# Turning attention probabilities in two row tiles of 64 queries, with ScalarE's copies moved ahead of the exponentials

## The chip, the cores and the metric

The kernel runs on one core of a Trainium2 chip. TensorE (PE in the profile) multiplies matrices and can write only to the accumulator memory (PSUM, eight banks per partition); VectorE (DVE) and ScalarE (ACT) do the element work and copy results out of PSUM; GpSimd (POOL) and SyncE (SP) mostly issue transfers. The metric is the device time of one execution in microseconds, the median of several runs. Less is better.

## The reference, cut to what matters

Attention over 4 batches and 8 heads (576 positions, head size 64, a bias computed from relative position), then a two-layer network with a smooth gate on the 2304 resulting rows of 512 numbers.

```python
scores = scale * np.matmul(q, k.transpose(0, 1, 3, 2)) + bias.transpose(2, 0, 1)[None, :, :, :]
scores = scores - np.max(scores, axis=-1, keepdims=True)
attn = np.exp(scores)
attn = attn / (np.sum(attn, axis=-1, keepdims=True) + 1e-09)
out = np.matmul(attn, v)
...
h = x @ w_in
sp = np.where(h > 20.0, h, np.log1p(np.exp(np.minimum(h, 20.0))))
g = h * np.tanh(sp)
return g @ w_out
```

The product `attn @ v` sums over the keys, so TensorE needs the probabilities with keys on the partitions, while the scores come out with queries on the partitions. Each block of probabilities is therefore transposed on TensorE. All of that is float32.

## The kernel before, in words

The kernel has three stages: a bias stage (up to about 64 us), the attention stage (about 64 to 320 us) and the network stage (to the end). The change is in the attention stage.

Attention works on 16 pairs of heads (4 pairs of heads times 4 batches). A pair takes five steps, one for each chunk of queries, in the order `ORDER = [0, 1, 4, 2, 3]`: four chunks `c < 4` of 128 queries, and chunk 4, which holds the last 64 queries of both heads in one tile. That makes 80 steps. Instructions are issued in the order in which the code is written, one queue per engine; engines wait for each other only through tiles and their buffers.

Step n issues, in this order:

- `scores(n)` (line 224): twelve TensorE matmuls for a chunk below 4. The two heads lie on partitions 0 to 63 and 64 to 127, so the matmuls of the two heads use two row tiles of 64 rows ("64*128" in the profile) and start side by side. Chunk 4 takes six matmuls over all 128 rows ("128*128").
- `add_bias(n)` (line 238): VectorE adds the bias and finds the row maximum, once per head, from PSUM tile `s` into `pt`. Tile `s` has two buffers, and a chunk below 4 uses both.
- `exps(n, 0)` and `exps(n, 1)` (line 253): ScalarE takes the exponentials in place in `pt`, with the row sums.
- `transposes(n - 2)` (lines 299 to 318): TensorE turns the probabilities of two steps earlier into PSUM tiles `tp` (three buffers of one bank each), and ScalarE copies them into `main` and `tail`. A chunk below 4 has eight main blocks of 128 queries by 128 keys (line 299) and one tail block (line 302); chunk 4 has four main blocks (line 311) and two small tails (lines 315 and 316). In every fifth step the reciprocals of the sums are turned as well (line 305).
- `pv_duo` (lines 331 and 335): TensorE multiplies `main` and `tail` with the values. The two heads use two column tiles of 64 columns ("128*64"). VectorE then copies the result `x` out (line 338).
- the work of later steps: loads, the split of q and k (line 191), and pieces of the conversion of network weights (lines 112 to 151).

In a transpose the block of probabilities is the stationary operand, which TensorE loads first (LDWEIGHTS, engine PEld in the profile), and the identity matrix `ident` is the moving operand. The rows of the block are the rows of the array that it occupies, and the number of moving columns equals the number of queries in the block.

Of the kernel before, what the change touches and what calls it, by code (L numbers as in the profile page):

```python
# [7 lines left out]
F32 = mybir.dt.float32  # L8
# [11 lines left out]
P = 128  # L20
# [24 lines left out]
def kernel(ctx: ExitStack, tc, qk, v, wb, w2, w_in, w_out, psia, psi4, rinv, eye, out):  # L45
    nc = tc.nc
    pe, dve, act, pool, sp = nc.tensor, nc.vector, nc.scalar, nc.gpsimd, nc.sync
# [23 lines left out]
    ident = const.tile([P, P], F32, name="ident")  # L71
# [143 lines left out]
    def scores(n):  # L215
        i, c = steps[n]
        hi, lo = qk_hi[i], qk_lo[i]
        live[n] = [s_ps.tile([P, 2, 512], F32, name="s") for _ in range(2 if c < 4 else 1)]
        for k, (stat, mov) in enumerate(((hi, hi), (hi, lo), (lo, hi))):
            for j in range(2):  # L220
                for h in range(2 if c < 4 else 1):
                    rows = slice(h * 64, h * 64 + 64) if c < 4 else slice(0, P)
                    k0 = KO + (0 if h else 64) + j * SH
                    pe.matmul(live[n][h][:, j, :SH], stat[rows, c * P:(c + 1) * P], mov[rows, k0:k0 + SH],  # L224
                              start=(k == 0), stop=(k == 2))

    def add_bias(n):

        i, c = steps[n]
        bt = bias_t[i // B, c]  # L230
        m = st.tile([P, 2], F32, name="m")
        if c < 4:
            pt = pp.tile([P, 2 * S], F32, name="pt")
        else:
            pt = p4p.tile([P, 640], F32, name="pt4")[:, :S]
        for u, s in enumerate(live[n]):
            sl = slice(u * S, (u + 1) * S)
            dve.tensor_tensor_reduce(  # L238
                out=halves(pt[:, sl]), in0=s[:, :, :SH], in1=halves(bt[:, sl]),
                scale=-0.125, scalar=BIG, op0=ALU.add, op1=ALU.min, accum_out=m[:, u:u + 1])  # L240
        live[n] = (pt, m)

    def exps(n, u):

        i, c = steps[n]
        if u == 1 and c == 4:
            return
        if i not in sums:
            sums[i] = st.tile([P, 9], F32, name="sums", bufs=3)
        pt, m = live[n]  # L250
        ps = pt[:, u * S:(u + 1) * S]
        k = 4 * u + c if c < 4 else 8
        act.activation(ps, ps, AF.Exp, bias=m[:, u:u + 1], scale=-1.0, accum_out=sums[i][:, k:k + 1])  # L253

    def reciprocals(i):

        r = sums.pop(i)
        dve.tensor_scalar(r, r, 1e-9, None, op0=ALU.add)
        dve.reciprocal(r, r)
        return r  # L260
# [3 lines left out]
    def store_reciprocals():  # L264
        i, tp = turned.pop()
        hp, b = divmod(i, B)
        rt = rt_first.pop() if rt_first else rt_tile()
        dve.tensor_copy(rt, tp[0:9, P:2 * P])
        sp.dma_start(out=r_d[b][hp], in_=rt)

    def pt_tiles(grp):
        w = 256 if grp == 0 else 320
        main = ptp.tile([P, 2, 4, w], F32, name=f"main{grp}")
        tail = tails[grp].pop() if tails.get(grp) else tail_tile(grp)
        return main, tail[:, :w]
# [7 lines left out]
    def x_tile():  # L283
        return xs.tile([P, 320], F32, name="x", bufs=2)

    def transposes(n):
        i, c = steps[n]
        pt, m = live.pop(n)
        grp = 0 if c < 2 else 1
        if (i, grp) not in pt_t:  # L290
            pt_t[i, grp] = pt_tiles(grp)
        main, tail = pt_t[i, grp]
        if c < 4:
            off = c * P if grp == 0 else 64 + (c - 2) * P
            for h in range(2):
                tp = t_ps.tile([P, 512], F32, name="tp")
                for k in range(4):
                    c0 = h * 640 + k * P
                    pe.transpose(tp[:, k * P:(k + 1) * P], pt[:, c0:c0 + P], ident)  # L299
                (dve.tensor_copy if n < 2 and h else act.copy)(main[:, h, :, off:off + P], tp.rearrange("p (k q) -> p k q", k=4))  # L300
            tp = t_ps.tile([P, 512], F32, name="tp")
            pe.transpose(tp[:, :P], pt[:, 512:640], ident)  # L302
            r = rc.pop(n, None)
            if r is not None:
                pe.transpose(tp[0:9, P:2 * P], r, ident)
                turned.append((i, tp))
            act.copy(tail[:, off:off + P], tp[:, :P])
        else:
            tp = t_ps.tile([P, 512], F32, name="tp")
            for k in range(4):  # L310
                pe.transpose(tp[:, k * P:(k + 1) * P], pt[:, k * P:(k + 1) * P], ident)  # L311
            act.copy(main[:, :, :, 0:64].rearrange("p h k q -> p k h q"),
                     tp.rearrange("p (k h q) -> p k h q", k=4, h=2))
            tp = t_ps.tile([P, 512], F32, name="tp")
            pe.transpose(tp[0:64, P:2 * P], pt[:, 512:S], ident)
            pe.transpose(tp[:, :P], pt[:, S - P:S], ident)
            act.copy(tail[0:64, 0:64], tp[0:64, P:P + 64])
            act.copy(tail[64:128, 0:64], tp[64:128, 64:128])
# [30 lines left out]
    blocks = [(0, 512), (512, 512), (1024, 256), (1280, 512), (1792, 512)]  # L349
# [25 lines left out]
    def ahead(n):  # L375

        i, x = divmod(n, 5)
        if x == (1 if i else 4) and i + 2 < NPAIR:
            load_hi(i + 2)
            load_raw(i + 2)  # L380
        if x == 4 and i + 2 < NPAIR:
            load_v(i + 2)
        if i % B == B - 1 and i // B + 1 < HP:
            load_bias(i // B + 1, ORDER[x])
        if n == NS - 11:
            load_x(0, x0)
        if n in (NS - 10, NS - 6):
            x_r[0] = x0.tile([P, 2, TB], F32, name="xr", bufs=1)
            h0 = 0 if n == NS - 10 else 2
            load_r(0, x_r[0], h0, h0 + 2)  # L390
        if n in (NS - 7, NS - 3):
            h0 = 0 if n == NS - 7 else 2
            for d in range(2):
                pool.tensor_tensor(x_raw[0][:, h0 + d], x_raw[0][:, h0 + d], x_r[0][:, d], op=ALU.mult)

    def split(n):

        i, x = divmod(n, 5)
        if (x == 2 or n == 3) and i + 1 < NPAIR:
            split_qk(i + 1)  # L400
        if w32:
            lower_weights(dve)
        if half:
            parts.pop(0)()
        elif n > 5 and w64[0][0] in order[:HALF]:
            scale_high(act if x == 2 else dve)
            parts.extend((shift_low, merge, lambda: (sign(), cast_weights())))

    def step(n):
        i, x = divmod(n, 5)  # L410
        late = n == 4

        def begin():
            if n < NS:
                scores(n)
                add_bias(n)
                exps(n, 0)

        def end():
            if n < NS:  # L420
                exps(n, 1)
                ahead(n)
            if 0 <= n - 1 < NS and (n - 1) % 5 == 4:
                rc[n - 1] = reciprocals((n - 1) // 5)
            if n < NS:
                split(n)
            if turned:
                store_reciprocals()


        if not late:
            begin()
        for k in {3: (0, 1)}.get(n, (n - LAG,)):
            if 0 <= k < NS:
                transposes(k)
        if not late:
            end()

        if late:
            for k in range(5):  # L440
                pv_duo(0, 0, k)
        for j, grp, ks in {4: ((i, 0, (0, 1)),), 0: ((i - 1, 0, (2, 3)),), 1: ((i - 1, 0, (4,)),),
                           2: ((i - 1, 1, (0, 1, 2)),), 3: ((i - 1, 1, (3, 4)),)}[x]:
            if 0 <= j < NPAIR and (j, grp) != (0, 0):
                for k in ks:
                    pv_duo(j, grp, k)
        if late:
            begin()
            end()
# [26 lines left out]
    def reach(t):  # L476

        left, right = 16 * t + 15, S - 16 * t
        n = max(left + 1, right)
        return left, right, n + n % 2  # L480
# [12 lines left out]
    for idx in range(NB + 2):  # L493
# [4 lines left out]
        if idx + 2 < NB:  # L498
            n = reach(ts[idx + 2])[2]
# [82 lines left out]
    t_ps = lpsum("t_ps", 3)  # L582
# [248 lines left out]
```

## Time and profile before

| what | value |
|---|---|
| median of 3 runs | 720.19 us (719.24 to 720.92) |
| the profiled execution | 721.65 us, span 719.7 us |
| TensorE busy | 697.3 us, 97% of the span |
| VectorE busy | 515.3 us, 72% |
| ScalarE busy | 467.2 us, 65% |
| granted TensorE clock, mean | 0.995 of full speed |

The span runs from the first to the last instruction. The time of the execution has about 2 us more around it. The profiled execution is 1.46 us above the median of the runs, so a sum made against the profile has to be carried over to the median.

### The profile page before, as it was taken

What the parts mean: (1) busy time and instruction counts of PE and PEld (TensorE: products, weight loads), DVE (VectorE), ACT (ScalarE), POOL (GpSimd) and SP (SyncE); (2) the same over time, 40 slices, a digit from 0 to 9 for tenths busy, and PEclk for the clock granted to TensorE, in tenths of its full rate; (3) what the DMA queues carried; (4) which work ended last, traced back from release to release, by engine and by line L of the source; (5) the groups of instructions that cost most, each with busy time, mean ns of one, the idle gap of its engine ahead of it and who ended that gap; (6) DMA issues with size and microseconds to landing.
All of it is one profiled execution on the core that took longest, in us unless ns stands there. A gap on an engine that the chain in (4) does not pass through costs nothing.

```text
span 719.7 us, 12986 instructions
## 1 busy us (share of the span) xinstructions
PE 697.3 (97%) x4880; PEld 532.4 (74%) x4880; DVE 515.3 (72%) x1051; ACT 467.2 (65%) x964; POOL 16.5 (2%) x26
## 2 busy tenths in 40 slices
PE   6988999999999999988999999999999999999997
PEld 3546776677677676656878888889988888888886
DVE  7894777777777876547888888775675567565564
ACT  6985888888888888845565565654554554454443
POOL 1000000000000001100000000000100000000000
PEclk9999999999999999999999999999999999999999
DMA  8989568548655844251113321214131000010001
GB/s 258 287 270 308 207 189 272 164 152 266 233 185 171 289 148 143 57 156 38 58 60 118 93 83 58 71 48 118 59 98 49 1 0 1 0 59 1 0 1 59
DMA packets 46430, 86.85 MB, mean 121 GB/s; under 512 B 13200, under 2 KB 22048, under 8 KB 46368
## 3 DMA queue, kind: packets, MB, share of 16 engines
q1 hardware_dynamic: 43488, 75.32, 32.5%
q0 software_dynamic: 2304, 10.49, 4.7%
q8 instruction: 38, 0.62, 0.4%
q10 hardware_dynamic: 576, 0.22, 0.1%
q14 instruction: 24, 0.20, 0.1%
HBM read 64.56 MB, written 21.45 MB: 120 GB/s over the span
## 4 chain that ended last, share of the span: by engine, by line
PE 86%; DVE 7%; ACT 4%; issue 1%; DMA 1%; DVEq 0%; ACTq 0%; SPq 0%
PE y L675 24%; PE h L630 24%; PE s L224 11%; PE o L331 9%; PE tp L299 8%; PE bps L528 5%; PE o L335 2%; PE tp L311 1%; PE tp L302 1%; DVE e L653 1%; DMA rawqk<-in_qk_dram 1%; DVE e L637 1%; DVE e L652 1%; ACT bt L534 1%; DVE w L127 1%
## 5 line engine op out<-in xcount | busy, mean ns | idle before, releaser
L253 ACT ACTIVATE pt<-pt,m 128x576 f32<-128x576 f32 x144 | 112.7, 782 | 40.8 <-DVE m L238 39.6
L238 DVE CUSTOM_DVE_ANT_0 pt<-s,bias 128x576 f32<-128x576 f32 x144 | 103.7, 753 | 47.4 <-PE s L224 47.4
L675 PE MATMUL y<-who,ghi 128*128 128x512 f32 x288 | 112.5, 391 | 2.2 <-ACT ghi L654 1.4
L675 PE MATMUL y<-who,glo 128*128 128x512 f32 x288 | 112.4, 390 | 1.0 <-DVE glo L657 1.0
L654 ACT CAST ghi<-e 128x512 fp32r<-128x512 f32 x72 | 44.7, 621 | 105.1 <-DVE e L653 101.9
L675 PE MATMUL y<-wlo,ghi 128*128 128x512 f32 x288 | 112.2, 390 | 0.0
L630 PE MATMUL h<-xhi,whi 128*128 128x512 f32 (+1 forms) x320 | 79.7, 369 | 1.3 <-ACT xhi L605 1.2
L657 DVE TENSOR_TENSOR glo<-e,ghi 128x512 fp32r<-128x512 f32 x72 | 49.7, 690 | 42.0 <-ACT ghi L654 42.0
L630 PE MATMUL h<-xlo,whi 128*128 128x512 f32 (+1 forms) x320 | 79.5, 371 | 0.0
L630 PE MATMUL h<-xhi,wli 128*128 128x512 f32 (+1 forms) x320 | 79.4, 370 | 0.0
L331 PE MATMUL o<-main,vt 128*64 128x320 f32 (+1 forms) x512 | 75.8, 418 | 0.8 <-DVE x L338 0.8
L635 ACT ACTIVATE e<-h 128x512 f32<-128x512 f32 x72 | 42.7, 592 | 46.2 <-PE h L630 46.2
L299 PE MATMUL tp<-ident,pt 128*128 128x128 f32 x512 | 70.0, 280 | 1.2 <-ACT main L300 1.2
L636 DVE TENSOR_SCALAR e<-e 128x512 f32<-128x512 f32 x72 | 30.6, 425 | 56.1 <-ACT e L635 56.1
L300 ACT COPY main<-tp 128x512 f32<-128x512 f32 x126 | 66.9, 581 | 1.0 <-PE tp L299 0.6
L630 PEld LDWEIGHTS h<-xhi,whi 128*128 128x128 f32 x320 | 57.3, 188 | 13.6 <-ACT xhi L605 2.7
L630 PEld LDWEIGHTS h<-xlo,whi 128*128 128x128 f32 x320 | 57.5, 190 | 10.2
L675 PEld LDWEIGHTS y<-who,ghi 128*128 128x128 f32 x288 | 54.1, 188 | 14.3 <-ACT ghi L654 2.2
L630 PEld LDWEIGHTS h<-xhi,wli 128*128 128x128 f32 x320 | 57.2, 190 | 10.1
L299 PEld LDWEIGHTS tp<-ident,pt 128*128 128x128 f32 x512 | 56.5, 142 | 10.3 <-issue 3.1
L675 PEld LDWEIGHTS y<-who,glo 128*128 128x128 f32 x288 | 54.1, 188 | 13.5 <-DVE glo L657 2.3
L675 PEld LDWEIGHTS y<-wlo,ghi 128*128 128x128 f32 x288 | 54.1, 188 | 10.9
(73 smaller groups left out, 1017.7 us busy)
## 6 DMA issues: line engine op xcount, KB each, us to landing
bias_d<-bt SPq DMA_DIRECT2D x36, 295.5 KB
qkhi<-in_qk_dram POOLq DMA_DIRECT2D x16, 640.0 KB, 6.2
rawqk<-in_qk_dram SPq DMA_DIRECT2D x16, 640.0 KB
w<-in_w_in_dram SPq DMA_DIRECT2D x16, 512.0 KB
w<-in_w_out_dram SPq DMA_DIRECT2D x16, 512.0 KB
vt<-in_v_dram SPq DMA_DIRECT2D x16, 320.0 KB
bias<-bias_d SPq DMA_DIRECT2D x16, 288.0 KB
out_dram<-w SPq DMA_DIRECT2D x17, 256.0 KB
```

The lines of the kernel that those rows point to most:

```text
L224: pe.matmul(live[n][h][:, j, :SH], stat[rows, c * P:(c + 1) * P], mov[rows, k0:k0 + SH], start=(k == 0), stop=(k == 2))
L238: dve.tensor_tensor_reduce(out=halves(pt[:, sl]), in0=s[:, :, :SH], in1=halves(bt[:, sl]), scale=-0.125, scalar=BIG, op0=ALU.add, op1=ALU. ...
L253: act.activation(ps, ps, AF.Exp, bias=m[:, u:u + 1], scale=-1.0, accum_out=sums[i][:, k:k + 1])
L299: pe.transpose(tp[:, k * P:(k + 1) * P], pt[:, c0:c0 + P], ident)
L300: (dve.tensor_copy if n < 2 and h else act.copy)(main[:, h, :, off:off + P], tp.rearrange("p (k q) -> p k q", k=4))
L331: pe.matmul(o[h * 64:h * 64 + 64, :w], vt[:, h, k, :], main[:, h, k, :], start=(k == 0), stop=False, **kw)
L528: pe.matmul(ps[cg * 32:cg * 32 + 32, a:b], w2t, src, start=True, stop=True)
L630: pe.matmul(h[:, u * n:(u + 1) * n], w["i", g4, d][:, r * P:(r + 1) * P], x[:, d, :n], start=(k == 0), stop=(k == 11))
L635: act.activation(e, h, AF.Exp)
L654: act.copy(ghi, e)
L657: dve.tensor_tensor(glo, e, ghi.bitcast(F32), op=ALU.subtract)
L675: pe.matmul(ys[blk][t], g[:, c0:c0 + P], w, start=((blk, f) in first and k == 0), stop=((blk, f) in last and k == 2))
```

## The change

Three things change. First, the main blocks are no longer turned 128 queries at a time: `turn_blocks` cuts each block into its upper 64 and its lower 64 queries, turns each half with a 64 by 64 piece of the identity, and puts the upper halves of all blocks into one `tp` tile and the lower halves into another. The halves alternate. Second, the copies out of the two `tp` tiles are now split by half instead of by head (for chunk 4, by head instead of all at once). Third, `exps(n, 0)` moves from the beginning of a step to its end, so ScalarE makes the copies of step n - 2 first and then both exponentials of step n.

```diff
+    ROWS = (slice(0, 64), slice(64, P))
+
+    def turn_blocks(pt, cols):
+
+        ab = [t_ps.tile([P, 512], F32, name="tp") for _ in ROWS]
+        for k, c0 in enumerate(cols):
+            for rows, tp in zip(ROWS, ab):
+                pe.transpose(tp[:, k * 64:(k + 1) * 64], pt[rows, c0:c0 + P], ident[rows, rows])
+        return [tp[:, :len(cols) * 64].rearrange("p (k q) -> p k q", q=64) for tp in ab]
+
     def transposes(n):
...
-            for h in range(2):
-                tp = t_ps.tile([P, 512], F32, name="tp")
-                for k in range(4):
-                    c0 = h * 640 + k * P
-                    pe.transpose(tp[:, k * P:(k + 1) * P], pt[:, c0:c0 + P], ident)
-                (dve.tensor_copy if n < 2 and h else act.copy)(main[:, h, :, off:off + P], tp.rearrange("p (k q) -> p k q", k=4))
+            blocks = main.rearrange("p h k q -> p (h k) q")
+            for u, tp in enumerate(turn_blocks(pt, [h * 640 + k * P for h in range(2) for k in range(4)])):
+                (dve.tensor_copy if n < 2 and u else act.copy)(blocks[:, :, off + 64 * u:off + 64 * u + 64], tp)
...
         else:
-            tp = t_ps.tile([P, 512], F32, name="tp")
-            for k in range(4):
-                pe.transpose(tp[:, k * P:(k + 1) * P], pt[:, k * P:(k + 1) * P], ident)
-            act.copy(main[:, :, :, 0:64].rearrange("p h k q -> p k h q"),
-                     tp.rearrange("p (k h q) -> p k h q", k=4, h=2))
+            for h, tp in enumerate(turn_blocks(pt, range(0, 512, P))):
+                act.copy(main[:, h, :, 0:64], tp)
...
                 scores(n)
                 add_bias(n)
-                exps(n, 0)
...
             if n < NS:
+                exps(n, 0)
                 exps(n, 1)
```

On TensorE, two neighbouring steps in the middle of the attention stage (a chunk below 4 being turned, then chunk 4) stand like this before. `s` are scores, `tp` turned blocks, `o` the product with the values; the shape is that of the output, and a product `o` counts once here although the profile shows two instructions for it.

```order
L224 MATMUL s<-qkhi,qklo 128x288 x4
L299 MATMUL tp<-ident,pt 128x128 x8
L302 MATMUL tp<-ident,pt 128x128
L331 MATMUL o<-main_3721,vt 64x320 x2
L335 MATMUL o<-tail_3722,vt 64x320 x2
...
L224 MATMUL s<-qkhi,qklo 128x288 x4
L311 MATMUL tp<-ident,pt_3854 128x128 x4
L315 MATMUL tp<-ident,pt_3854 64x128
L316 MATMUL tp<-ident,pt_3854 128x128
```

With the change the same place reads as follows.

```order
L224 MATMUL s<-qkhi,qklo 128x288 x4
L293 MATMUL tp<-ident,pt 128x64 x16
L309 MATMUL tp<-ident,pt 128x128
L335 MATMUL o<-main_4154,vt 64x320 x2
L339 MATMUL o<-tail_4155,vt 64x320 x2
...
L224 MATMUL s<-qkhi,qklo 128x288 x4
L293 MATMUL tp<-ident,pt_4310 128x64 x8
L319 MATMUL tp<-ident,pt_4310 64x128
L320 MATMUL tp<-ident,pt_4310 128x128
```

Eight transposes over 128 rows became sixteen over 64 rows with half as many moving columns (and four became eight); their place between the scores and the tail is the same.

On ScalarE, two steps in the same part of the program stand like this before (`pt` lines are exponentials, `main` and `tail` lines copies).

```order
L253 ACTIVATE pt,sums<-pt,m 128x576
L300 COPY main_4177<-tp 128x4x128 x2
L307 COPY tail_4178<-tp 128x128
L253 ACTIVATE pt,sums<-pt,m 128x576 x2
L300 COPY main_4177<-tp 128x4x128 x2
L307 COPY tail_4178<-tp 128x128
L253 ACTIVATE pt,sums<-pt,m 128x576
```

With the change, the corresponding steps of a neighbouring pair read as follows.

```order
L307 COPY main_4686<-tp 128x8x64 x2
L314 COPY tail_4687<-tp 128x128
L253 ACTIVATE pt,sums<-pt,m 128x576 x2
L307 COPY main_4686<-tp 128x8x64 x2
L314 COPY tail_4687<-tp 128x128
L253 ACTIVATE pt,sums<-pt,m 128x576 x2
```

The first exponential of a step moved behind the step's three copies. Each copy of `main` still moves 512 elements per partition, now as eight runs of 64 instead of four of 128.

## Rows read from the trace of the kernel before

**Rows 1.** The page: TensorE's busy time, share of span, instructions.

```profile
PE 697.3 (97%) x4880; PEld 532.4 (74%) x4880; DVE 515.3 (72%) x1051; ACT 467.2 (65%) x964; POOL 16.5 (2%) x26
```

**Rows 2.** Busy time by stretch: length, engines, granted clock, DMA share, GB/s.

```profile
68.00:306.00 238.00, 237.79 (x2041) 167.15 (x2038) 175.10 (x435) 202.25 (x514) 11.39 (x16) 0.99 0.59 193
326.00:719.00 393.00, 386.27 (x1786) 321.43 (x1784) 278.68 (x460) 203.62 (x341) 2.60 (x2) 1.00 0.15 49
```

**Rows 3.** Timeline of TensorE, two steps: start us, us, instruction, count.

```profile
200.96 0.43 PE L224 MATMUL s<-qkhi,qklo 128*128 128x288 f32 x2
201.22 1.03 PE L299 MATMUL tp<-ident,pt 128*128 128x128 f32 x8
202.09 0.27 PE L302 MATMUL tp<-ident,pt 128*128 128x128 f32 x1
...
204.09 0.53 PE L224 MATMUL s<-qkhi 64*128 64x288 f32 x4
204.47 0.42 PE L224 MATMUL s<-qklo,qkhi 64*128 64x288 f32 x4
204.73 0.42 PE L224 MATMUL s<-qkhi,qklo 64*128 64x288 f32 x4
205.08 1.09 PE L299 MATMUL tp<-ident,pt 128*128 128x128 f32 x8
206.01 0.27 PE L302 MATMUL tp<-ident,pt 128*128 128x128 f32 x1
206.22 0.76 PE L331 MATMUL o<-main,vt 128*64 128x320 f32 x4
206.81 0.71 PE L335 MATMUL o<-tail,vt 128*64 128x320 f32 x4
207.44 0.53 PE L224 MATMUL s<-qkhi 64*128 64x288 f32 x4
```

**Rows 4.** The same timeline, a product of 256 moving columns.

```profile
209.25 1.08 PE L331 MATMUL o<-main,vt 128*64 128x256 f32 x8
210.26 0.53 PE L224 MATMUL s<-qkhi 64*128 64x288 f32 x4
```

**Rows 5.** The same timeline, tail block and then nine columns of reciprocals.

```profile
215.33 0.27 PE L302 MATMUL tp<-ident,pt 128*128 128x128 f32 x1
215.44 0.27 PE L305 MATMUL tp<-ident,sums 128*9 128x128 f32 x1
```

**Rows 6.** Timeline of weight loads: first and second of two kinds of scores, second transpose.

```profile
200.32 0.30 PEld L224 LDWEIGHTS s<-qkhi 128*128 128x128 f32 x2 [0.38 <-DVE m L238]
200.43 0.19 PEld L224 LDWEIGHTS s<-qkhi 128*128 128x128 f32 x1
...
204.20 0.19 PEld L224 LDWEIGHTS s<-qkhi 64*128 64x128 f32 x2
...
205.14 0.14 PEld L299 LDWEIGHTS tp<-ident,pt 128*128 128x128 f32 x1
```

**Rows 7.** Groups of instructions: the main transposes; count, busy us, mean ns, idle.

```profile
L299 PE MATMUL tp<-ident,pt 128*128 128x128 f32 x512 | 70.0, 280 | 1.2 <-ACT main L300 1.2
```

**Rows 8.** Timeline of ScalarE in one step without waiting.

```profile
186.95 0.78 ACT L253 ACTIVATE pt<-pt,m 128x576 f32<-128x576 f32 x1
...
187.72 1.05 ACT L300 COPY main<-tp 128x512 f32<-128x512 f32 x2
188.67 0.28 ACT L307 COPY tail<-tp 128x128 f32<-128x128 f32 x1
```

**Rows 9.** Timeline of VectorE: both heads' bias in one step.

```profile
205.19 0.76 DVE L238 CUSTOM_DVE_ANT_0 pt<-s,bias 128x576 f32<-128x576 f32 x1 [0.50 <-PE s L224]
...
206.55 0.08 DVE L238 DVE_READ_ACCUMULATOR2_ANT m<- 128x1 f32 x1
```

**Rows 10.** Waits from 75 to 325 us: who for whom, us, times, longest.

```profile
ACT pt L253 <- DVE m L238: 32.3, 56, 1.3
```

**Rows 11.** Timeline of TensorE at the end of the attention stage.

```profile
308.93 2.06 PE L630 MATMUL h<-xhi,whi 128*128 128x512 f32 x4 [1.22 <-ACT xhi L605]
```

## The prediction

> **What bounds the kernel now.** First the page: TensorE is busy for 97% of the span [rows 1]. Then the busy times by stretch, since an average hides stages. From 68 to 306 us, where the change lies, TensorE is busy for 237.79 of 238.00 us, ScalarE for 202.25 and VectorE for 175.10, at a granted clock of 0.99 [rows 2]; from 326 us on nothing changes. These 238 us are 15 pairs of heads, 15.87 us each. A busy TensorE may still be a waiting one, because the time of a matmul is longer than its place in the array. So the third view is TensorE's timeline: one must look at when the next instruction starts, not at how long one takes. There the step's instructions follow each other without a wait for another engine [rows 3]. What TensorE's queue loses or gains in this stage is therefore the first estimate of the result, until ScalarE or VectorE cannot follow.
>
> **What a main transpose costs today.** Eight start at 201.22 and the tail at 202.09: 0.109 us each [rows 3]. The price goes by the moving columns. The tail, with the same 128 moving columns, also holds the array for 0.11 us although the load behind it has only nine columns [rows 5], so the weight loads are hidden. A product over two column tiles says the same: 320 moving columns take 1.22 us for four pairs (206.22 to 207.44), 256 take 1.01 us (209.25 to 210.26) [rows 3, 4], so 64 float32 columns cost 0.053 us per pair, and two tiles pay it together.
>
> **What a pair of halves will cost.** No row shows a float32 transpose in row tiles, so both its parts are bounded. Do two row tiles run side by side? The scores do: four over 64 rows take 0.26 us (204.47 to 204.73), as do two over 128 rows (200.96 to 201.22) [rows 3]. So a pair of halves has 64 moving columns to pay once, 0.053 to 0.055 us. The loads: the second transpose's load starts 0.06 us after the first (205.08, 205.14) [rows 3, 6], which is what one full load of float32 takes when nothing hides it. Do two half-height loads take as long as one full one? For scores they do: the second full load starts 0.11 us after the first (200.32, 200.43), and with two row tiles the second pair starts 0.11 us after the first pair (204.09, 204.20) [rows 3, 6]. I take a price p of 0.058 us per pair, between the columns (0.055) and the load (0.060). The lower end is 0.053; the upper end, with loads or matmuls strictly one after another, 0.11 to 0.12.
>
> **Where the switch of tile shape goes.** Transposes over 128 rows start 0.09 us late behind scores over 64 rows (205.08 instead of 204.73 + 0.26), and their first load adds 0.06 us (0.93 us for eight, 206.01 - 205.08, against 0.87); behind scores over 128 rows neither appears [rows 3]. I price a switch at 0.15 us. The Trainium skill, page "TensorEngine Tiling (Array Packing)", section Key Properties, says that changing the tiling mode drains TensorE; by that rule too, the 128-row tail behind the 64-row halves pays for a switch. The trace agrees, with the 0.09 us; were the tail's switch free, the sum below would be 80 x 0.15 = 12 us larger. So:
> - Blocks of chunks 0 (at their own place, below), 1, 2 and 3: for the three that follow 64-row scores, the switch moves from ahead of the main blocks to behind them. Gain 0.87 - 8p, 48 times.
> - Chunk 0 is turned behind the 128-row scores of chunk 4, where there is no switch now and will be two. Gain 0.87 - 8p - 0.30, 16 times.
> - Chunk 4, four blocks: 0.436 - 4p, 16 times.
>
> Together the 80 steps give 57.9 - 576p us: **24.5 us at p = 0.058**, 27.4 at 0.053, nothing at 0.10, and 5.5 to 11 us lost at 0.11 to 0.12. The 512 records of line 299 [rows 7] are the 64 eights in it.
>
> **ScalarE.** Its copies of 512 elements keep their price (1.05 us for two, 0.28 for the tail [rows 8]), in runs of 64 instead of 128. For chunk 4 one copy becomes two of 256 elements, each between 0.28 and 0.53 us; at 0.36 each that is 0.2 us more per pair of heads, 3 us in all on ScalarE. The moved exponential costs nothing by itself. Today ScalarE waits 32.3 us for VectorE's maximum, 56 times [rows 10], with the copies queued behind that wait; now the copies fill that time. The exponentials finish later in their step, but are read two steps later. A step's work is two exponentials of 0.78 us at most and copies of 1.33 us at most, 2.9 us with all overlaps counted twice; the mean over the stretch has to do: 202.25 + 3 us of work in 238 - 24.5 = 213.5 us, 96%. Part of the 202 us is the start-up of instructions after the 56 waits, which goes with them. It fits, but barely, and it is the cover under which the gain stands: without it a lag of ScalarE reaches TensorE through the `tp` buffers. Both halves now need two free banks before the first pair, where the second bank was needed four blocks later.
>
> **VectorE.** The scores of the next step need both buffers of `s`. A step's scores start at 204.09, VectorE starts at 205.19 and is done with both heads at 206.63 [rows 3, 9]: a loop of 2.54 us. The step from 207.44 to 210.26 [rows 3, 4], which turns chunk 4, shrinks from 2.82 to 2.62 us, still above the loop; the shortest step is followed by chunk 4's scores, which need one buffer alone. No loss here, but no more than 0.1 us of room either.
>
> **Ends of the stage.** The last steps are held by ScalarE (the network's first matmul waits 1.22 us for it [rows 11]), not by transposes; I take off 1 us, and 1.5 us for steps in which ScalarE is late. Gain 22 us.
>
> **The rivals.**
> - *ScalarE sets the pace.* If half of its 32.3 us of waits stays, now as waits for `tp`, its 205 us grow to 221, and only 17 of the 238 us go; less the ends, the median would be about 706. For it speaks the 96%; against it, that the copies no longer stand behind the maximum. It decides from about 0.1 us of waiting per step on.
> - *Loads are not hidden behind matmuls of the same rows.* Then today's 0.109 is a load of 0.055 and a matmul of 0.054, and a pair becomes 0.055 + 0.027 = 0.082: a gain of 10.7 us, less 1.5, about 711. The nine-column load [rows 5] speaks against it, since the block ahead of it should then have been followed after 0.06 us. The rule is that of the Trainium skill, page "TensorE: Matmul & The Clock Gate", section The mechanism: a weight load overlaps running matmuls only where the row group differs. The trace does not agree, with the 0.11 us of those rows.
> - *The halves do not overlap (the other side).* If float32 loads of two row tiles go one after the other, p is 0.11 to 0.12, sixteen loads bound the group, and the two switches at chunk 4's scores come on top: 5.5 to 11 us slower, 726 to 731. It decides from p = 0.10 on. For it speaks that no row has such float32 transposes; against it the scores, whose loads and matmuls overlap in both tiles.
>
> **How the numbers follow.** The span of 719.7 us becomes 697.7, the profiled execution's 721.65 becomes 699.65; the median of the runs lay 1.46 us below that execution, so I say 698.2 us. For this case alone, p from 0.053 to 0.065 gives 695 to 702. Chances: the forecast 0.70, ScalarE's pace 0.13, unhidden loads 0.06, no overlap 0.11. The range from 693.5 to 711 holds the first, nearly all of the second and half of the third, a little over 8 in 10. A measurement of this kernel tells about 0.2% (1.4 us) from no change: faster 0.87, same 0.03 (from the edges of the last two cases), slower 0.10.
>
> **What would show it.** In the profile after: eight pairs of halves in 0.44 to 0.52 us from the first to the switch; no gap between 64-row scores and the first half, and 0.15 us ahead of the tail; a pair of heads in about 14.3 us; ScalarE's waits for VectorE's maximum mostly gone and its busy share near 95%. A pair of halves at 0.11 us, TensorE waiting for `tp` copies in most steps, or scores waiting for VectorE's maximum would make it wrong.

## The result and the profile after

The changed kernel takes **699.89 us** (698.39 to 701.45), the kernel before 720.56 us (719.24 to 721.03) in the same comparison: a ratio of 0.9716, 95% interval 0.9691 to 0.9742, 20.7 us faster. The profiled execution took 701.45 us, with a span of 699.5 us against 719.7.

The page of the changed kernel, as in [rows 1], with its groups of ScalarE's exponentials and main copies (count, busy us, mean ns, idle time ahead and what ended most of it):

```profile
PE 675.6 (97%) x5456; PEld 515.5 (74%) x5456; DVE 514.3 (74%) x1051; ACT 463.9 (66%) x980; POOL 16.5 (2%) x26
...
L253 ACT ACTIVATE pt<-pt,m 128x576 f32<-128x576 f32 x144 | 112.5, 792 | 6.5 <-DVE m L238 6.2
...
L307 ACT COPY main<-tp 128x512 f32<-128x512 f32 x126 | 68.1, 597 | 18.4 <-PE tp L293 18.0
```

TensorE has 576 instructions more and 21.7 us less busy time. ScalarE's 32.3 us of waits for VectorE's maximum [rows 10] are down to 6.2 us; it now waits for the halves instead (18.0 us), as an engine with work to spare does.

Busy time by stretch, as in [rows 2]: the attention stage from 68 us, now to 284 us; the rest of the kernel; and the start of the stage:

```profile
68.00:284.00 216.00, 215.74 (x2572) 150.91 (x2572) 172.68 (x434) 198.47 (x525) 11.41 (x16) 0.98 0.65 212
304.00:699.00 395.00, 388.05 (x1794) 322.92 (x1793) 279.58 (x462) 204.68 (x343) 2.60 (x2) 1.00 0.15 49
54.00:75.00 21.00, 16.04 (x176) 12.72 (x169) 10.39 (x26) 10.89 (x29) 0.53 (x1) 0.84 0.97 324
```

TensorE is still busy in all of the stage, and behind the stage nothing changed. In this execution the start of the stage lost something; it is read further down.

TensorE's timeline in two steps of the changed kernel, the same places of the loop as in [rows 3]:

```profile
190.45 0.43 PE L224 MATMUL s<-qkhi,qklo 128*128 128x288 f32 x2
190.81 0.71 PE L293 MATMUL tp<-ident,pt 64*128 64x64 f32 x16
191.45 0.33 PE L309 MATMUL tp<-ident,pt 128*128 128x128 f32 x1
191.71 1.83 PE L335 MATMUL o<-main,vt 128*64 128x320 f32 x12
193.47 0.53 PE L224 MATMUL s<-qkhi 64*128 64x288 f32 x4
193.84 0.42 PE L224 MATMUL s<-qklo,qkhi 64*128 64x288 f32 x4
194.11 0.43 PE L224 MATMUL s<-qkhi,qklo 64*128 64x288 f32 x4
194.37 0.66 PE L293 MATMUL tp<-ident,pt 64*128 64x64 f32 x16
194.96 0.33 PE L309 MATMUL tp<-ident,pt 128*128 128x128 f32 x1
195.21 0.76 PE L335 MATMUL o<-main,vt 128*64 128x320 f32 x4
195.80 0.71 PE L339 MATMUL o<-tail,vt 128*64 128x320 f32 x4
196.44 0.53 PE L224 MATMUL s<-qkhi 64*128 64x288 f32 x4
```

Read the starts. A half is one transpose of 64 queries, and a pair is one half in each row tile. Behind 64-row scores the halves follow without a gap (194.11 + 0.26 = 194.37). The sixteen starts lie within 0.435 us, seven intervals of 0.062 us, and the tail starts 0.154 us after the last pair, one interval and 0.09 us of switch: 0.59 us in all. Behind 128-row scores (190.45) there is the switch too: 0.36 us to the halves instead of 0.26, and 0.64 us from the first half to the tail, 0.05 of it the first load. The step from 193.47 to 196.44 takes 2.97 us, where it took 3.35 (204.09 to 207.44 in [rows 3]).

Why 0.062 us: the last pair of the group at 190.81, its loads and its matmuls, changed kernel:

```profile
191.24 0.14 PEld L293 LDWEIGHTS tp<-ident,pt 64*128 64x128 f32 x2
191.29 0.23 PE L293 MATMUL tp<-ident,pt 64*128 64x64 f32 x2
```

A half's load starts some 0.005 us after the matmul ahead of it (191.23, one interval before 191.29), and its own matmul follows about 0.055 us later. So I read that loads, not columns, set the pace; no run changes one without the other. The first two pairs of loads of that group start 0.056 us apart with nothing to hide them, where two full loads start 0.06 us apart (205.08 and 205.14 in [rows 3, 6]): loads of both tiles together take what one full load takes.

ScalarE's timeline in the same step of the changed kernel:

```profile
193.11 0.84 ACT L253 ACTIVATE pt<-pt,m 128x576 f32<-128x576 f32 x1
...
195.06 1.07 ACT L307 COPY main<-tp 128x512 f32<-128x512 f32 x2 [1.01 <-PE tp L293]
196.01 0.28 ACT L314 COPY tail<-tp 128x128 f32<-128x128 f32 x1
196.17 0.80 ACT L253 ACTIVATE pt<-pt,m 128x576 f32<-128x576 f32 x1
```

The copies come first and wait 1.01 us for the halves, and the exponential follows the tail's copy at once: the maximum has long been there.

### The profile page after: what moved, and what is told of

It is laid out like the page before. It is cut to its first block, busy times and chain, and to the rows that moved or that the text cites. A ratio compares the mean times of both kernels' runs of the same rounds, so it can differ in the third digit from the quotient of the medians.

```text
span 699.5 us, 14139 instructions
## 1 busy us (share of the span) xinstructions
PE 675.6 (97%) x5456; PEld 515.5 (74%) x5456; DVE 514.3 (74%) x1051; ACT 463.9 (66%) x980; POOL 16.5 (2%) x26
## 4 chain that ended last, share of the span: by engine, by line
PE 85%; DVE 7%; ACT 3%; DMA 3%; issue 1%; SPq 0%; DVEq 0%; ACTq 0%
PE y L679 25%; PE h L634 24%; PE s L224 11%; PE o L335 10%; PE tp L293 5%; PE bps L532 5%; PE o L339 2%; PE tp L309 2%; DMA rawqk<-in_qk_dram 1%; DMA xlo<-r_d 1%; DVE e L657 1%; DVE e L641 1%; DVE e L656 1%; ACT bt L538 1%; DVE w L127 1%
## 5 line engine op out<-in xcount | busy, mean ns | idle before, releaser
L657 DVE TENSOR_TENSOR e<-e,r 128x512 f32<-128x512 f32 x72 | 49.9, 693 | 7.5
L224 PEld LDWEIGHTS s<-qkhi 64*128 64x128 f32 (+1 forms) x288 | 25.0, 189 | 36.9 <-DVE m L238 16.2
```

What stands on the lines that cost most here:

```text
L657: dve.tensor_tensor(e, e, r, op=ALU.mult)
```

## The experiments

Each ratio is to the kernel before, timed on the same chip; the runs are spread over several chips, so ratios are compared and not only times. The theory: two row tiles turn a pair of blocks in about the time of one load, and ScalarE's new order is what lets it follow. The rivals differ by run.

**1. The tiles without the new order.** In the changed kernel:

```diff
                 add_bias(n)
+                exps(n, 0)
 ...
-                exps(n, 0)
                 exps(n, 1)
```

> The row tiles as in the change, but the first exponential of a step stands ahead of the copies again, as before the change. Theory (TensorE's queue sets the pace, and the moved exponential is the cover under which ScalarE can follow): ScalarE waits for VectorE's maximum ahead of the copies again, 32 us of waits beside some 200 us of work do not fit into the 216 us that TensorE now leaves, so TensorE waits for copies and part of the gain is lost: 704 to 716 us. Rival (the order costs nothing, only the tiles count): 699 to 701 us.

Measured 711.57 us (709.26 to 712.63), 0.9883 [0.9852, 0.9914], in the theory's range. The new order is worth 12 of the 20.7 us; a pair of heads takes 15.11 us here and 14.40 in the changed kernel. The waits of this kernel from 75 to 292 us (who for whom, us, times, longest):

```profile
ACT pt L253 <- DVE m L238: 23.3, 37, 1.5
...
PEld tp L293 <- ACT main L307: 7.9, 26, 0.4
```

and TensorE's timeline in one of its steps:

```profile
208.30 0.27 PE L293 MATMUL tp<-ident,pt 64*128 64x64 f32 x1
208.79 0.71 PE L293 MATMUL tp<-ident,pt 64*128 64x64 f32 x15 [0.21 <-ACT main L307]
```

ScalarE waits for the maximum again, its copies behind that wait are late, and the lateness comes out at the halves: the first has its bank, its partner in the other tile waits for the second bank, and fourteen wait behind it. That both banks are wanted before the first pair is the new sensitive point.

**2. The new order without the tiles.** The same line moved the other way, in the kernel before.

> The transposes as before the change, only the first exponential moved behind the copies. Theory (TensorE's queue is full without it, so ScalarE's order has nothing to give): 719 to 722 us, with ScalarE's waits for VectorE's maximum mostly gone all the same. Rival (the order carries a good part of the gain): 705 to 716 us.

Measured 720.18 us (717.31 to 721.73), 0.9995 [0.9976, 1.0015]: nothing, as the theory says. A pair of heads takes 15.85 us as before. The waits of this kernel from 75 to 295 us:

```profile
ACT main L300 <- PE tp L299: 23.8, 31, 1.9
...
ACT main L312 <- PE tp L311: 7.2, 11, 0.7
```

ScalarE's wait of 32.3 us for the maximum [rows 10] has become 31.0 us for the transposes. This wait belongs to an engine that does not set the pace, and moving it cost and gave nothing. With the tiles it counts, because ScalarE then has 22 us less for the same work.

**3. The same halves, all of one tile first.** In `turn_blocks` of the changed kernel:

```diff
-        for k, c0 in enumerate(cols):
-            for rows, tp in zip(ROWS, ab):
+        for rows, tp in zip(ROWS, ab):
+            for k, c0 in enumerate(cols):
```

> The change, but all upper halves are turned first and all lower halves after them, instead of alternating: the same instructions in another order. Theory (the gain is that loads and matmuls of two row tiles run side by side): neighbours now share a row tile, sixteen loads follow each other at about 0.06 us, a group takes 0.99 us instead of 0.49, and 64 x 0.5 + 16 x 0.25 = 36 us come on top: 726 to 738 us. Rival (half the moving columns give half the price whatever the order, or TensorE overlaps them by looking ahead in its queue): 699 to 702 us.

Measured 718.4 us (715.27 to 719.84), 0.997 [0.9949, 0.9991]: between the ranges of the two. TensorE's timeline of one group of this kernel:

```profile
156.89 0.42 PE L224 MATMUL s<-qkhi,qklo 64*128 64x288 f32 x4
157.15 0.96 PE L293 MATMUL tp<-ident,pt 64*128 64x64 f32 x16
158.04 0.33 PE L309 MATMUL tp<-ident,pt 128*128 128x128 f32 x1
```

From the first half to the tail 0.89 us instead of 0.59: strictly one after another it would be 16 x 0.062 + 0.09 = 1.08 us. So three pairs still ran together (starts in the order of the program would allow one, the last of the upper tile with the first of the lower). The single starts of this group, in us after the first:

```
0 .055 .118 .181 .242 .248* .304 .361 .365 .423 .428 .486 .550 .612 .674 .739
```

The starts come in twos in the middle only. The one with the star takes 273 ns, where others take some 220, and lies 0.25 us after the first in the groups behind 64-row scores (0.30 where the first load is exposed). I read it as the first half of the lower tile, ninth in the program, because a tile's first half is the one that must wait for its bank: in 59 of the 64 groups of sixteen, this sixth start and the first one are the only ones that carry such a wait. So it starts with the fifth of the upper tile, ahead of the sixth to the eighth.

**4. Four of one tile, then four of the other.** In the changed kernel's `turn_blocks`:

```diff
-        for k, c0 in enumerate(cols):
+        for k4 in range(0, len(cols), 4):
             for rows, tp in zip(ROWS, ab):
+                for k, c0 in list(enumerate(cols))[k4:k4 + 4]:
```

> The change, with the halves issued four upper, four lower, four upper, four lower, instead of alternating. All eight upper ones first had cost 0.74 us for a group instead of 0.43, with the first lower half starting beside the fifth upper one. Theory (TensorE starts a matmul of the other row tile ahead of its turn when it stands up to four matmuls behind): the four lower ones start at once beside the upper ones, and the time is that of the change, 699 to 702 us. Rival (neighbours in the queue must alternate, and the overlap seen in the sequence of eight came from the end of the first tile's work): every four run alone, a group takes about 0.9 us, 722 to 732 us.

Measured 701.87 us (700.82 to 703.33), 0.9755 [0.9727, 0.9782], at the upper edge of the theory's range. TensorE's timeline of one group of this kernel:

```profile
184.38 0.72 PE L294 MATMUL tp<-ident,pt 64*128 64x64 f32 x16
185.02 0.33 PE L310 MATMUL tp<-ident,pt 128*128 128x128 f32 x1
```

0.64 us to the tail, one interval more than alternating. A pair of heads takes 14.69 us instead of 14.40, so the time is not quite that of the change: 4.8 us for sixteen pairs by the steps, 2.8 us by the ratios. Here the first half of the lower tile, fifth in the program, starts with the first of the upper (0.007 us later). Both runs fit a TensorE that starts the first matmul of the other row tile together with the one four places ahead of it in the program, while the three between them still wait. The Trainium skill, page "TensorE: Matmul & The Clock Gate", section The mechanism, has matmuls start and end strictly in the order of the program; for starts in different row tiles these two traces do not agree, by the 0.739 and 0.494 us within which the sixteen starts lie.

**5. Chunk 0's tail turned first**, behind the 128-row scores of chunk 4, which spares one of the two switches there. In `transposes` of the changed kernel:

```diff
+            if c:
+                turn_main()
             tp = t_ps.tile([P, 512], F32, name="tp")
             pe.transpose(tp[:, :P], pt[:, 512:640], ident)
 ...
             act.copy(tail[:, off:off + P], tp[:, :P])
+            if not c:
+                turn_main()
```

> The change, but where the main blocks follow chunk 4's scores over 128 rows (chunk 0's blocks, once per pair of heads), the tail block over 128 rows is turned first and the halves after it. Theory (each change of tile shape costs TensorE about 0.15 us): one switch less per pair of heads, 16 x 0.15 = 2.4 us less, 697 to 698.5 us. Rivals: the switch is free, then 699 to 701 us; or the last of the three banks, which now takes a half, comes free too late, then 700 to 703 us.

Measured 698.57 us (695.82 to 699.36), 0.9702 [0.9674, 0.973], between the ranges of the theory and of a free switch. The same kernel again, beside the changed kernel on one chip:

> The tail first behind chunk 4's scores, once more. Theory (one switch of tile shape less in each of 16 pairs of heads; the steps in the trace were shorter by 0.15 us): 2.4 us below the change on the same chip, 696 to 699.5 us. Rival (what the steps gain is lost at the ends of the stage): within 1 us of the change.

> The changed kernel once more, as it is, to stand on the same chip beside the version with the tail first. Theory: 698 to 702 us.

Measured 697.56 us (696.29 to 698.95), 0.9691 [0.9666, 0.9716], against 698.86 us (697.23 to 701.23), 0.9713 [0.9688, 0.9737] for the change. TensorE's timeline of two such steps, in the first of these runs:

```profile
131.67 0.27 PE L314 MATMUL tp<-ident,pt 128*128 128x128 f32 x1
131.87 0.90 PE L293 MATMUL tp<-ident,pt 64*128 64x64 f32 x16
132.71 1.84 PE L342 MATMUL o<-main,vt 128*64 128x320 f32 x12
...
203.03 0.43 PE L224 MATMUL s<-qkhi,qklo 128*128 128x288 f32 x2
203.29 0.27 PE L314 MATMUL tp<-ident,pt 128*128 128x128 f32 x1
203.49 0.71 PE L293 MATMUL tp<-ident,pt 64*128 64x64 f32 x16
204.13 1.84 PE L342 MATMUL o<-main,vt 128*64 128x320 f32 x12
205.90 0.53 PE L224 MATMUL s<-qkhi 64*128 64x288 f32 x4
```

The tail follows the 128-row scores without a gap (203.03 + 0.26). From these scores to the next step it takes 2.87 us, where the change takes 3.02 (190.45 to 193.47): one switch of 0.15 us less, as priced. Of the fourteen pairs of heads from the third on, eleven have it, and their step goes from 3.66 to 3.51 us. In the other three, as at 131.87, the halves take 0.84 us to the product instead of 0.64, and the step takes 3.70 us. VectorE's copies of the reciprocals in these two steps, same run, say why:

```profile
131.74 0.27 DVE L268 COPY rt<-tp 9x128 f32<-9x128 f32 x1
...
203.07 0.28 DVE L268 COPY rt<-tp 9x128 f32<-9x128 f32 x1 [0.24 <-ACT tail L319]
```

The reciprocals stand in the third `tp` bank of the step before, which with the tail first goes to the lower halves. At 203 the copy ends at 203.35, before the halves begin (203.49). At 131 it ends at 132.01: the first upper half has started at 131.87, and its partner starts at 132.06. All three late steps show this, in run 7 and in the second comparison too, so the rival of the bank that comes free too late holds in three pairs of fourteen. The mean gain is then 0.10 us per pair, 1.7 us for sixteen and not 2.4. The times show 1.3 in both comparisons, whose intervals overlap with the change's: the saving is seen in the steps, not settled in the time. This version has the lowest median of all that ran.

**6. The raw load of the second pair of heads asked for earlier.** At the start of the stage VectorE waits for a transfer. In the changed kernel:

```diff
+        if idx == 33:
+            load_raw(1)
         if idx == NB:
-            load_raw(1)
             load_v(1)
```

> The change, with one transfer moved: the q and k of the second pair of heads (rawqk) are requested three rounds earlier in the bias stage. Theory (the first microseconds that the tiles save are lost again because VectorE waits 5.04 us for that transfer at the start of the attention stage, and TensorE 3.44 us for VectorE): 696 to 699 us. Rival (the transfer engines are full at that time, so that an earlier request only pushes others back): 699 to 702 us.

Measured 702.53 us (699.88 to 706.41), 0.9768 [0.9738, 0.9799]: no gain, half a microsecond above the rival's range, and the theory of a request that comes too late has fallen. This kernel's window at the start of the stage:

```profile
54.00:75.00 21.00, 17.27 (x161) 12.69 (x154) 9.19 (x22) 9.67 (x25) 0.53 (x1) 0.70 0.86 285
```

The request went out at 54.19 instead of 57.26 us and VectorE's wait for it is down to 1.4 us, but other transfers are now late (a copy of ScalarE waits 2.3 us for a store of the bias stage, VectorE 1.2 us for the bias), and the clock granted in these 21 us is 0.70 instead of 0.84. The DMA engines of the changed kernel were 0.97 busy there, so I read that what is asked for sooner takes its turn from something else.

With the fifth edit as well:

> Both together: the tail first behind chunk 4's scores, and the transfer requested earlier. Theory (the two are independent, 2.4 us of switches and 1 to 4 us of start): 694 to 697.5 us. Rival (neither start nor switch adds to the other, or the transfer gives nothing): 698 to 701 us.

Measured 700.08 us (697.75 to 703.16), 0.973 [0.9701, 0.9758], in the rival's range. Its waits from 53 to 75 us have the bias too:

```profile
DVE pt L238 <- DMA bias<-bias_d: 2.5, 2, 1.4
```

**7. More work for ScalarE.** How near is it to setting the pace? The copy of the lower half made twice, in the changed kernel:

```diff
                 (dve.tensor_copy if n < 2 and u else act.copy)(blocks[...], tp)
+                if n >= 2 and u:
+                    act.copy(blocks[...], tp)
```

> The change, with the copy of the lower halves of every chunk below 4 (from the third step on) made twice by ScalarE, with the same result: some 62 x 0.48 = 30 us more work on ScalarE and nothing else. Theory (ScalarE is the next bound, with 198.5 us of work in the 216 us of the stage): 17.5 us of it are free, the rest lands on the time, 710 to 718 us. Rival (ScalarE still has room or the waits move elsewhere): 699 to 703 us.

Measured 722.31 us (719.04 to 724.88), 1.0035 [1.0016, 1.0055]: the mechanism of the theory, but above its range. This kernel's busy times from 75 to 290 us, and two of its waits from 75 to 295 us:

```profile
75.00:290.00 215.00, 204.67 (x2357) 138.69 (x2357) 162.84 (x400) 210.91 (x536) 9.76 (x14) 1.00 0.60 198
```

```profile
PEld tp L293 <- ACT main L309: 15.3, 29, 1.0
PE tp L293 <- ACT main L309: 9.8, 23, 0.8
```

ScalarE is busy for 98% and TensorE waits for its copies: the two rows, of loads and of matmuls, show the same waits and are not to be added. The 62 added copies made ScalarE's busy time in the stage 33.9 us longer (249.5 against 215.6 us) and the kernel 22.4 us, so some 11 us were free, not the 17.5 us (216.0 - 198.5) that the windows seem to offer. A share of 92% is a mean over five kinds of step, and ScalarE's room is not spread evenly: the step that turns chunk 0 went from 3.66 to 4.34 us (4.86 in every fourth pair of heads) and the one that turns chunk 3 from 2.43 to 3.00, while the other three grew by less than 0.1.

## Why the prediction was right

**The place and the mechanism held.** What TensorE's queue loses is the result, within 3 us: its steps lose 23.4 us (below), the time 20.7. The two rivals on the tiles are excluded by the spacing of the pairs: 0.062 us, neither 0.082 (loads unhidden) nor 0.11 to 0.12 (no overlap). ScalarE's pace is excluded as a bound of the change: in the steady steps TensorE hardly waits for a copy, and a pair of heads takes 14.40 us where 14.3 was forecast. But run 1 shows that this rival is near: without the new order the time is 711.57 us.

**The price of a switch held.** 0.15 us was read from a switch that the change moves (0.09 and a first load of 0.06); after it is 0.09 ahead of the tail, with a first load of 0.05 to 0.06, and run 5 takes one away and sees 0.15 go.

**The price of a pair, 0.058 us, was too low: 0.062.** The load at 0.060 was the nearer bound, and I put the value between the load and the columns. The sum 57.9 - 576p becomes 22.2 us, 2.3 less. The steps themselves gave a little more than that: by their place in a pair of heads, starting with chunk 4's scores, they went from 3.75 to 3.66, 3.35 to 2.97, 2.81 to 2.58, 3.14 to 2.76 and 2.81 to 2.43 us, together 1.46 per pair, or 0.29 per step and 23.4 us for 80, where the formula with 0.062 gives 22.2. Of these 1.2 us, 0.5 stand in the step that turns chunk 4 (2.81 to 2.58): the block behind its halves has 64 stationary columns instead of 128, and its first load delays it by 0.03 us (the next matmul starts 0.135 us after it, less 0.109) where the price of a switch has 0.06, sixteen times. The rest is open.

**The 1.5 us for steps in which ScalarE is late were not lost there, and the ends of the stage kept back more than 1 us.** The scores of step 79 start at 282.81 instead of 302.58 us; chunk 4's scores in the second pair of heads (step 7) start at 74.30 instead of 72.97. So the 72 steps between saved 21.1 us (0.29 each). Ahead of them five steps' blocks are turned, and 1.3 us were lost where 1.5 should have been saved, 2.8 us short. Behind them three are turned, and 0.4 us came back instead of 0.9: 24.5 - 2.3 + 1.2 - 2.8 - 0.4 = 20.2 us of span. The timeline of VectorE and TensorE at the start of the stage, changed kernel:

```profile
65.03 1.49 DVE L191 TENSOR_TENSOR qklo<-rawqk,qkhi 128x1280 fp32r<-128x1280 f32 x1 [5.04 <-DMA rawqk<-in_qk_dram]
...
67.59 0.40 PE L224 MATMUL s<-qkhi 64*128 64x288 f32 x1 [3.44 <-DVE m L238]
```

and the same instruction of VectorE in the kernel before, with its window from 54 to 75 us:

```profile
64.03 1.49 DVE L191 TENSOR_TENSOR qklo<-rawqk,qkhi 128x1280 fp32r<-128x1280 f32 x1 [2.56 <-DMA rawqk<-in_qk_dram]
```

```profile
54.00:75.00 21.00, 17.42 (x151) 13.37 (x143) 10.86 (x27) 12.27 (x31) 0.53 (x1) 0.92 0.96 320
```

In this execution VectorE waits in its queue for a transfer that lands 1.0 us later than before, and the bias behind it, the maximum and the scores wait with it; the granted clock in these 21 us is 0.84 instead of 0.92. But that is one execution of each kernel. The changed kernel's second profile, of run 5's comparison, shows the same transfer and the same scores (the last line):

```profile
62.97 1.49 DVE L191 TENSOR_TENSOR qklo<-rawqk,qkhi 128x1280 fp32r<-128x1280 f32 x1 [3.12 <-DMA rawqk<-in_qk_dram]
...
71.89 0.38 PE L224 MATMUL s<-qkhi 128*128 128x288 f32 x1
```

There the transfer lands 1.1 us earlier than in the kernel before, chunk 4's scores start 1.1 us earlier, and the clock is 0.92; run 2's kernel, which turns its blocks as before, has these scores at 71.03. So the start moves by 2 us and more between executions, and the 1.3 us lost here are not shown to be the change's. What two comparisons do show is a time 20.7 and 20.8 us shorter, where 80 steps at the steady saving give 23.4: about 2.7 us stay behind at the two ends of the stage, and which wait keeps them is open. Runs 6 and 7 show that asking earlier does not bring them: their scores start at 76.06 and 75.73 us, later than in every other profile.

**Part of the closeness is luck.** The sum had p too low (2.3 us too much) and missed 1.2 us of the steps; the 2.5 us taken off were to cover late steps of ScalarE and the last steps, and what they happened to cover lies in part at the start, of which the forecast said nothing.

**ScalarE's share is 92%, not 96%.** Its busy time fell from 202.25 to 198.47 us although chunk 4 has a copy more: I read that the start-ups after 56 waits went with the waits, which the forecast named and did not take off. Neighbouring instructions now overlap more: over thirteen pairs of heads their durations add up to 221.7 us within 174.3 us of busy time, before to 213.4 within 177.0. The split copies cost 0.38 us each, 0.36 was taken.

The end of the stage is as it was: the network's first matmul waits 1.27 us for ScalarE, 1.22 before [rows 11]. TensorE's timeline there, changed kernel:

```profile
288.65 2.35 PE L634 MATMUL h<-xhi,whi 128*128 128x512 f32 x4 [1.27 <-ACT xhi L609]
```

## What to carry to other kernels

Where a matmul's price goes by its moving columns, two row tiles with half the columns each can bring it towards half, down to the time of one weight load: take that load as the price, read from two loads of the same kind with nothing to hide them (0.06 us for the blocks here, 0.11 for the scores' [rows 6]), and count each change of tile shape on both sides. A gain on the engine that sets the pace is kept only if the engine that empties its banks can follow: here the reorder of ScalarE's queue was worth nothing alone and 12 of 21 us together with the tiles. A stage that waits for transfers at its start, with full DMA engines, may keep back some of what is saved; how much cannot be read from one pair of profiles.

## What the runs showed that was not expected

- TensorE started matmuls of one row tile ahead of up to three earlier ones of the other tile: in sequence of eight the sixteen starts lie within 0.739 us, in fours within 0.494, alternating within 0.435.
- Float32 transposes in two row tiles, 64 queries each, take 0.062 us per pair, against 0.109 us for one transpose of a full block; this is read as the pace of their loads.
- An engine with 92% of a stage busy took some 11 us of added work, not 17.5, before the rest of it went into the time.
- The first microseconds of the attention stage differ by 2 us and more between executions, largely with when one transfer lands (62.97 to 65.03 us).
